# Attention and a mixture of experts on one core: some transposes of the probabilities moved from the DMA to TensorE

## The chip, the core and the metric

One core of a Trainium2 chip runs the whole program. The metric is the device time of one execution in microseconds, as the median of several runs. The engines that matter: TensorE (PE; its weight loads are listed as PEld), VectorE (DVE), ScalarE (ACT), GpSimd (POOL), and SyncE (SP), on whose queue all DMAs of the stage told of here are issued.

## The reference

```python
def _attn_ref(q, k, v, w1, b1, w2):          # B, H, S, D = 4, 8, 576, 64
    scores = scale * np.matmul(q, k.transpose(0, 1, 3, 2))
    ...                                      # a small network of the positions gives bias
    scores = scores + bias.transpose(2, 0, 1)[None, :, :, :]
    scores = scores - np.max(scores, axis=-1, keepdims=True)
    attn = np.exp(scores)
    attn = attn / (np.sum(attn, axis=-1, keepdims=True) + 1e-09)
    return np.matmul(attn, v).astype(np.float32)

def _moe_ref(x, w_gate, w1, w2):             # N, D, E, F = 2304, 512, 8, 1024
    logits = x @ w_gate
    logits = logits - logits.max()
    P = np.exp(logits)
    for _ in range(8):
        P /= P.sum(1, keepdims=True) + 1e-09
        P /= P.sum(0, keepdims=True) + 1e-09
        P *= N / E
    out = np.zeros((N, D), dtype=np.float32)
    for e in range(E):
        h = np.maximum(x @ w1[e], 0.0)
        ye = h @ w2[e]
        out += P[:, e:e + 1] * ye
```

## The kernel before, in words

The first part of the program computes the attention, the second the experts. The products run in pairs of f16 numbers (a high and a low half), so that the sums come out as in f32.

Attention goes by 16 **units**: one of the 4 batches with one of the 4 pairs of heads. The 576 query rows of a unit are five groups for each head: four tiles of 128 rows for each of the two heads, and one last tile that holds the 64 remaining rows of both. A unit is worked off in five **steps** (`unit_steps`): `gi` 0 and 1 are two pairs of tiles, once for each head `hh` (two tiles a step), and `gi` 2 is the last, fifth tile (one tile). The first four units do their steps of `gi` 0 first and then the rest; from the fifth unit on, a unit's five steps follow each other. There are 80 steps.

A step of two tiles does this. TensorE writes the scores of a tile into `s`, a PSUM tile of two buffers (`ps_s`). VectorE adds the bias and takes the maximum on the way to `sb` (tiles `br`, `bt` are the bias). ScalarE takes the exponential and its sum in place. `st_rcp` makes the reciprocal on VectorE. `st_hi` scales `sb` to f16 on ScalarE: the high half of `ah`. `st_lo` computes the low half on VectorE and issues the **DMA transpose** that turns `ah` (128 x 1152 for one tile, in blocks of 128 x 128: 9 blocks a tile) into `aT`. `ah` has 2 buffers, `aT` 3 for steps of two tiles, and 1 (`aT4`) for the fifth tile. Two steps after `st_lo` (`LAG`), `attend` multiplies `aT` with the values `vs` (or `xb`) into `pv`, from which ScalarE and VectorE make `xa`, `xb`, `xc`, the input of the experts.

Beside this run: loads of the next units' `nat` tiles, their cut into halves (`qk`, `vs`) and the transposes of `qk` on TensorE into `l` (`u_trans`, f16, identity `id16`), copied to `qkT`; and the first expert's matmuls, `l<-...,area`, which fill TensorE where it would wait.

What sets the order: every instruction of this part is recorded by `Engine` objects with a cost that the code estimates, and `Plan.emit` then writes them out by a list schedule over those costs: at each time the engine that is free first takes its ready work, in order of priority and then of the recording. `as_one` keeps a group together. Engines run their list in order. As every operation goes through one recording line, the profile shows L210 for all of them; tiles tell them apart. In the second part, a second plan does the same for the gate, the scaling of `P` and the experts.

Of the kernel before, what the change touches and what calls it, by code (L numbers as in the profile page):

```python
# [9 lines left out]
F16 = mybir.dt.float16  # L10
# [8 lines left out]
P = 128  # L19
B, H, S, D = 4, 8, 576, 64  # L20
NHP = H // 2
# [249 lines left out]
def attention_sinkhorn_moe(ctx, tc, q, k, v, w1, b1, w2, wg, m1, m2, xm, xm4, xf, sel, out):  # L271
# [11 lines left out]
    plan = Plan()  # L283
    vec, act, pool, pe, sync = (
        Engine(plan, e, n)
        for e, n in ((nc.vector, "dve"), (nc.scalar, "act"), (nc.gpsimd, "pool"), (nc.tensor, "pe"), (nc.sync, "dma"))
    )
# [15 lines left out]
    id16 = consts.tile([P, P], F16, name="id16")  # L303
# [109 lines left out]
    with ExitStack() as actx:  # L413
# [35 lines left out]
        def ps_s():  # L449
            return psA.tile([P, 1024], F32, name="ps_s", tag="s", bufs=2)  # L450
# [68 lines left out]
        for kind in range(1, 4):  # L519
            vec.scalar_tensor_tensor(  # L520
                out=wr,
# [8 lines left out]
            out=wa.rearrange("p g (j k) -> p (g j) k", j=4),  # L530
# [92 lines left out]
        def bias_step(between=()):  # L623
# [27 lines left out]
            out=w1r, in0=pw[:, H : H + 2], scalar1=s_wb[:, 0:1], scalar2=2.0**-11, op0=ALU.mult, op1=ALU.mult  # L651
# [5 lines left out]
            out=w2m,  # L657
# [22 lines left out]
        for i in range(2):  # L680
            r = slice(32 * i, 32 * i + 1)
# [113 lines left out]
        for n in range(8):  # L795
            for m in (2 * n, 2 * n + 1):
                nm, _, i = qk_order[m]
# [9 lines left out]
        with plan.urgent():  # L807
# [6 lines left out]
            out=c8, in0=u_qk[:, 0:1], scalar=0.125, in1=u_qk[:, 1:2], op0=ALU.mult, op1=ALU.mult  # L814
# [7 lines left out]
            out=g, in0=g0, scalar=s_qk[:, 0:1], in1=s_qk[:, 1:2], op0=ALU.mult, op1=ALU.mult  # L822
# [140 lines left out]
        def st_lo(s):  # L963
            n, ah = len(s["sb"]), s["ah"]
            s["aT"] = wrk.tile([P, 9 * n, P], F16, name="aT", tag="aT" if n == 2 else "aT4", bufs=3 if n == 2 else 1)
            for i, sb in enumerate(s["sb"]):
                vec.scalar_tensor_tensor(
                    out=ah[:, i, S:],
                    in0=sb,
                    scalar=s["st"][:, 3, i : i + 1],  # L970
                    in1=ah[:, i, 0:S],
                    op0=ALU.mult,
                    op1=ALU.subtract,
                )
            sync.dma_start_transpose(out=s["aT"], in_=ah.rearrange("p n s -> p (n s)"))

        def attend(u, gi, ss):

# [158 lines left out]
        for n in range(NS + LAG + 1):  # L1137
# [19 lines left out]
            if 0 < n <= NS:  # L1157
                s = steps[n - 1]
                st_hi(s)
                st_lo(s)  # L1160
                u, gi, hh = s["key"]
                groups.setdefault((u, gi), []).append(s)
                if gi == 2 or hh == 1:
                    due.append((n + LAG, u, gi, groups.pop((u, gi))))
# [21 lines left out]
        vec, act, pool, pe, sync = nc.vector, nc.scalar, nc.gpsimd, nc.tensor, nc.sync  # L1186
# [682 lines left out]
    for n, (e, b) in enumerate(seq):  # L1869
        r = visit[n]  # L1870
        i, at_end, leaves = (b, r % 2), n % 5 == 4, visit[n + 1 : n + 2] != [r]
# [96 lines left out]
```

## Time and profile before

| | us |
|---|---|
| median of 3 runs | 1784.25 |
| lowest, highest | 1779.7, 1787.0 |
| the profiled execution | 1784.56 |
| its span, first to last instruction | 1782.8 |

| engine | busy us | share of the span |
|---|---|---|
| PE | 1686.8 | 95% |
| DVE | 1447.8 | 81% |
| ACT | 1086.3 | 61% |
| POOL | 78.7 | 4% |

These shares are averages over two parts that have different limits. They are read by stage: the share of each engine and of the 16 DMA engines in stretches of the span, then the waits in the stretch in question, then the chain of work that ended last there. The attention part lasts until about 517 us, the experts take the rest.

### The profile page before, as it was taken

To read this page: it belongs to the slowest core of one execution; us is meant where nothing else is said; L and a number is where in the kernel's file an instruction comes from. 1 tells how busy PE (TensorE), PEld (TensorE's weight loads), DVE (VectorE), ACT (ScalarE), POOL (GpSimd) and SP (SyncE) were. 2 spreads that over 40 slices of the span, in tenths; PEclk is the share of its full clock that TensorE was granted. 3 is DMA by queue.
4 is the path that set the end of the run, shared out by engine and by line. 5 is a ranking of instruction groups with operands and counts; after the bars stand their busy time and mean duration, and the time that the engine had idled before them with its cause. 6 is when DMAs were issued, how large, how long until landed. Compare 5 with 4: busy or idle time off the path is not lost.

```text
span 1782.8 us, 40479 instructions
## 1 busy us (share of the span) xinstructions
PE 1686.8 (95%) x16640; PEld 1377.4 (77%) x16640; DVE 1447.8 (81%) x2627; ACT 1086.3 (61%) x1930; POOL 78.7 (4%) x90
## 2 busy tenths in 40 slices
PE   7887897898989999999999999999999999999998
PEld 4544564555666688888988898889888988898887
DVE  6898988898968898778887787878788878876666
ACT  7887888888856675545564555565555544453443
POOL 0120012122200000000000000000000000000000
PEclk9988799999999999999999999999999999999999
DMA  7769999999993164644473557445545653463321
GB/s 259 240 160 225 206 196 200 200 201 194 202 268 136 68 204 181 231 165 163 170 279 135 201 190 248 154 143 213 214 173 180 237 192 131 160 238 103 104 73 37
DMA packets 303358, 324.24 MB, mean 182 GB/s; under 512 B 191420, under 2 KB 231876, under 8 KB 298180
## 3 DMA queue, kind: packets, MB, share of 16 engines
q1 hardware_dynamic: 303172, 321.65, 60.0%
q8 instruction: 130, 2.13, 0.5%
q14 instruction: 56, 0.46, 0.1%
HBM read 189.86 MB, written 88.08 MB: 156 GB/s over the span
## 4 chain that ended last, share of the span: by engine, by line
PE 78%; DVE 8%; DMA 7%; ACT 3%; issue 2%; SPq 0%; DVEq 0%; ACTq 0%
PE bankA L1591 18%; PE bankA L1611 13%; PE bankE L1591 9%; PE bankE L1611 9%; PE bankB L1611 9%; PE l L210 6%; PE bankB L1591 4%; DMA aT<-ah 4%; PE s L210 4%; PE pv L210 3%; ACT area L210 2%; DVE ah L210 1%; DVE area L210 1%; DVE sb L210 1%; PE bankS L1427 1%
## 5 line engine op out<-in xcount | busy, mean ns | idle before, releaser
L1591 PEld LDWEIGHTS <-slot 128*128 128x128 f16 x5040 | 450.7, 98 | 48.3 <-issue 2.5
L1611 PEld LDWEIGHTS <-hA 128*128 128x128 f16 x2268 | 222.4, 98 | 27.1 <-issue 0.6
L210 PEld LDWEIGHTS <-area 128*128 128x128 f16 (+1 forms) x2477 | 155.2, 101 | 101.5 <-issue 33.2
L1591 PE MATMUL bankA<-xt,slot 128*128 128x256 f16 (+1 forms) x1680 | 186.1, 262 | 0.2 <-ACT u L1648 0.2
L1591 PE MATMUL bankE<-xt,slot 128*128 128x256 f16 (+1 forms) x1680 | 186.1, 262 | 0.0
L1636 ACT ACTIVATE hA<-c 128x512 f16<-128x512 f32 x189 | 118.0, 627 | 111.3 <-DVE c L1214 110.4
L1611 PEld LDWEIGHTS <-hS 128*128 128x128 f16 x1512 | 147.2, 98 | 22.2 <-ACT hS L1636 3.0
L1611 PEld LDWEIGHTS <-area 128*128 128x128 f16 x1512 | 148.0, 98 | 18.5 <-issue 1.4
L210 DVE SCALAR_TENSOR_TENSOR ah<-sb,st,ah 128x576 f16<-128x576 f32 x144 | 122.4, 876 | 24.1 <-ACT ah L210 23.9
L1214 DVE SCALAR_TENSOR_TENSOR hA<-c,hA 128x512 f16<-128x512 f32 x189 | 127.5, 685 | 12.3 <-ACT hA L1636 10.2
L1695 ACT COPY u<-bankA 128x512 f32<-128x512 f32 (+1 forms) x70 | 37.8, 540 | 157.6 <-PE bankA L1611 157.4
L210 ACT ACTIVATE ah<-sb,st 128x576 f16<-128x576 f32 x144 | 106.2, 770 | 37.6 <-DMA aT<-ah 33.5
L1648 ACT ACTIVATE u<-bankA 128x512 f32<-128x512 f32 x126 | 75.1, 596 | 67.6 <-PE bankA L1591 63.8
L210 ACT ACTIVATE sb<-sb,st 128x576 f32<-128x576 f32 x144 | 110.4, 769 | 7.4 <-DVE st L210 7.1
L210 PE MATMUL l<-area 128*128 128x512 f16 (+1 forms) x413 | 110.6, 385 | 3.5 <-ACT ys L210 0.4
L1214 DVE SCALAR_TENSOR_TENSOR acc<-c,fs,acc 128x256 f32<-128x256 f32 x252 | 110.6, 480 | 2.1 <-DMA out_dram<-acc 0.2
L210 PE MATMUL s<-qkT 128*128 128x512 f16 (+3 forms) x560 | 84.5, 302 | 23.0 <-DVE st L210 22.1
L1611 PE MATMUL bankA<-area,hS 128*128 128x256 f16 x756 | 88.6, 273 | 3.2 <-ACT hS L1636 2.5
L1611 PE MATMUL bankA<-area,hA 128*128 128x256 f16 x756 | 89.8, 276 | 0.0
L1611 PE MATMUL bankA<-area 128*128 128x256 f16 x756 | 88.2, 273 | 1.0 <-ACT u L1695 1.0
L1611 PE MATMUL bankE<-area,hS 128*128 128x256 f16 x756 | 88.5, 273 | 0.0
L1611 PE MATMUL bankB<-area,hA 128*128 128x256 f16 x756 | 88.2, 273 | 0.0
(239 smaller groups left out, 3155.6 us busy)
## 6 DMA issues: line engine op xcount, KB each, us to landing
sc_w<-stage SPq DMA_DIRECT2D x84, 512.0 KB
acc<-sc_y SPq DMA_DIRECT2D x102, 256.0 KB
area<-sc_w SPq DMA_DIRECT2D x48, 512.0 KB
sc_y<-acc SPq DMA_DIRECT2D x84, 256.0 KB
xt<-sc_t SPq DMA_DIRECT2D x18, 1024.0 KB
slot<-sc_w SPq DMA_DIRECT2D x36, 512.0 KB
bt<-sc_bias SPq DMA_DIRECT2D x26, 576.0 KB
raw<-in_moe_w_dram SPq DMA_DIRECT2D x28, 512.0 KB
```

Source lines behind the costliest of these rows:

```text
L210: self.plan.record(self.name, cost, lambda: fn(*args, **kw), ins, outs, move)
L1214: vec.scalar_tensor_tensor(out=o, in0=x, scalar=s, in1=y, op0=op0, op1=op1)
L1427: pe.matmul(r, id16 if sg > 0 else nid16, v[:, a, 2 * dq : 2 * dq + 2, tok * w : tok * w + w], start=(j == 0), stop=(j == len(seq_) - 1),)
L1591: pe.matmul(ps[:, jf * w : jf * w + w], t[:, a, c * 512 + f * P : c * 512 + f * P + P], x(xp, c), start=(first and jf == 0 and c == 0 and ...
L1611: pe.matmul(ps[:, j * 256 : j * 256 + 256], h[:, a, fc * w + j * P : fc * w + j * P + P], t[:, wp, fc * 256 : fc * 256 + 256], start=(firs ...
L1636: on_act(0.58, lambda: act.activation(h[:, 0, sl], x, AF.Relu if relu else AF.Copy), [r], wk)
L1648: on_act(0.55, lambda: act.activation(tmp[k], bank[b], f, scale=HS), [b], [k], 0)
L1695: on_act(0.27 * nt, lambda: act.copy(tmp[k][:, :n], bank[b][:, :n]), [b], [k], 0)
```

## The change

In `st_lo`, the DMA transpose stays only for some steps. For the fifth tile of every unit (`gi == 2`), and for the first four units' step with `(gi, hh) == (1, 1)`, whose two tiles are the last pair of the second head, each tile is transposed by nine matmuls with the identity into one buffer of `s` (taken as f16), and copied to `aT` by two instructions: ScalarE takes five blocks (640 columns), VectorE four (512 columns). That is 20 of the 80 steps and 24 tiles.

```diff
-            sync.dma_start_transpose(out=s["aT"], in_=ah.rearrange("p n s -> p (n s)"))
+            u, gi, hh = s["key"]
+            if not (gi == 2 or u < NHP and (gi, hh) == (1, 1)):
+                sync.dma_start_transpose(out=s["aT"], in_=ah.rearrange("p n s -> p (n s)"))
+                return
+            for i in range(n):
+                ps = ps_s().bitcast(F16)[:, : 9 * P].rearrange("p (r x) -> p r x", x=P)
+                with plan.as_one():
+                    for r in range(9):
+                        pe.transpose(ps[:, r], ah[:, i, r * P : (r + 1) * P], id16)
+                act.copy(s["aT"][:, 9 * i : 9 * i + 5], ps[:, :5])
+                vec.tensor_copy(s["aT"][:, 9 * i + 5 : 9 * i + 9], ps[:, 5:])
```

The plan orders everything behind the first such step anew. Three places show how. In the rows, the number behind a tile's name tells its buffer: `s_116` and `s_118` are the two of `s`.

TensorE, at the first unit's step `(1, 1)`, which is the first place where the orders part. Before, behind the last matmul of a `pv` group:

```order
L210 MATMUL pv_112<-aT_138,xb 64x256
L210 LDWEIGHTS qkT_129
L210 MATMUL s_116<-qkT_129 128x512
L210 LDWEIGHTS qkT_129
L210 MATMUL s_116<-qkT_129 128x64
```

Now, at the same place (nine transposes into each buffer, the repeats left out):

```order
L210 MATMUL pv_112<-aT_138,xb 64x256
L210 LDWEIGHTS ah_144
L210 MATMUL s_116<-id_68,ah_144 128x128
...
L210 LDWEIGHTS ah_144
L210 MATMUL s_118<-id_68,ah_144 128x128
...
L210 LDWEIGHTS qkT_129
L210 MATMUL s_116<-qkT_129 128x512
```

The scores that followed the `pv` group now stand behind 18 transposes, which use both buffers of `s` in turn.

VectorE at the same place, as a piece of the difference:

```order
 L210 ISA st_135 128x1
 L210 SCALAR_TENSOR_TENSOR xa<-pv_112,xa 128x256
+L210 COPY aT_124<-s_116 128x512
+L210 SCALAR_TENSOR_TENSOR area<-area,sms 128x1024
+L210 COPY aT_124<-s_118 128x512
 L210 ISA sb_141,st_139<-s_116,bt_123,sms 128x576
 L210 ISA st_139 128x1
 L210 ISA sb_133,st_139<-s_118,bt_123,sms 128x576
```

The two copies, with a cut of the first expert's weights between them, now stand ahead of the maxima (`ISA sb`) of the next scores, which use the same buffers.

SP, from the fourth unit's fifth tile through the fifth unit. Before:

```order
L210 DMA_TRANSPOSE aT_0_117<-ah_144 128x9x128
L210 DMA sc_y<-ys_108 128x512
L210 DMA bt_121<-sc_bias 128x1152
L210 DMA_TRANSPOSE aT_138<-ah_142 128x18x128
L210 DMA bt_123<-sc_bias 128x1152
L210 DMA_TRANSPOSE aT_122<-ah_144 128x18x128
L210 DMA sc_y<-ys_108 128x512
L210 DMA_TRANSPOSE aT_124<-ah_142 128x18x128
L210 DMA nat_119<-in_v_dram 64x2x64
L210 DMA nat_120<-in_q_dram 64x2x256 x2
L210 DMA_TRANSPOSE aT_138<-ah_144 128x18x128
```

Now:

```order
L210 DMA bt_121<-sc_bias 128x1152
L210 DMA_TRANSPOSE aT_122<-ah_144 128x18x128
L210 DMA bt_123<-sc_bias 128x1152
L210 DMA_TRANSPOSE aT_124<-ah_142 128x18x128
L210 DMA nat_119<-in_q_dram 64x2x256
L210 DMA_TRANSPOSE aT_138<-ah_144 128x18x128
L210 DMA sc_y<-ys_108 128x512
L210 DMA nat_119<-in_q_dram 64x2x256
L210 DMA nat_119<-in_q_dram 128x64
L210 DMA nat_120<-in_k_dram 128x576
L210 DMA_TRANSPOSE aT_122<-ah_142 128x18x128
```

The transposes of 9 blocks (`aT_0`) are gone from SP's list, the four of 18 blocks of the unit stay, and the loads between them have moved. From the gate matmuls at the end of the attention part on, the orders of all engines are the same.

## Rows read from the trace of the kernel before

**Rows 1.** The page's 40 slices of 44.6 us: busy tenths, DMA share in tenths.

```profile
PE   7887897898989999999999999999999999999998
...
DMA  7769999999993164644473557445545653463321
```

**Rows 2.** Stretches: length, PE, PEld, DVE, ACT, POOL busy (instructions), clock, DMA share, GB/s.

```profile
185.00:240.00 55.00, 47.83 (x459) 29.94 (x458) 51.43 (x108) 46.51 (x92) 7.08 (x7) 0.89 0.88 183
215.00:240.00 25.00, 24.40 (x259) 15.27 (x254) 22.62 (x49) 20.69 (x44) 5.44 (x4) 1.00 0.77 145
220.00:240.00 20.00, 19.40 (x194) 11.92 (x193) 19.23 (x39) 17.55 (x39) 5.44 (x4) 1.00 0.80 151
240.00:285.00 45.00, 42.44 (x412) 26.95 (x411) 38.84 (x89) 36.92 (x75) 9.22 (x11) 1.00 0.97 213
285.00:325.00 40.00, 28.07 (x277) 16.91 (x276) 34.60 (x80) 33.25 (x67) 7.34 (x9) 0.83 0.98 193
325.00:500.00 175.00, 161.69 (x1624) 104.62 (x1622) 156.09 (x348) 146.11 (x298) 35.63 (x35) 1.00 0.95 197
500.00:517.00 17.00, 15.64 (x178) 11.58 (x177) 6.14 (x9) 8.13 (x15) 0.00 (x0) 1.00 0.94 253
```

**Rows 3.** Waits, 240 to 500 us: engine, tile <- releaser: us in total, times, longest.

```profile
ACT ah L210 <- DMA aT<-ah: 21.1, 20, 2.2
DVE ah L210 <- ACT ah L210: 17.4, 17, 2.5
PE s L210 <- DVE st L210: 17.1, 22, 1.8
...
PE pv L210 <- DMA aT<-ah: 6.5, 7, 2.6
```

**Rows 4.** Chain that ended last, 185 to 517 us: by line, and one of its pieces (start, us).

```profile
by line: PE l L210 27.5%; DMA aT<-ah 23.1%; PE pv L210 13.9%; PE s L210 9.6%; DVE ah L210 6.0%; issue 4.8%; DVE sb L210 3.2%; ACT ah L210 2.3%; DVE area L210 2.1%; ACT sb L210 1.1%; DVE qk L210 0.9%; DVE st L210 0.8%; ACT area L210 0.8%; DV
...
268.65 5.04 DMA aT<-ah
```

**Rows 5.** Waits, 215 to 240 us, columns as in rows 3.

```profile
DVE ah L210 <- ACT ah L210: 0.9, 2, 0.8
...
ACT ah L210 <- DMA aT<-ah: 0.5, 1, 0.5
```

**Rows 6.** DMA transposes on SP's queue: all (ns), two small ones; 185-517 us traffic.

```profile
L210 SPq DMA_TRANSPOSE aT<-ah x80: 1253/3078/6224, 94.2 to 509.4; - x80
...
351.11 1.39 SPq L210 DMA_TRANSPOSE aT<-ah  x1
...
373.18 1.32 SPq L210 DMA_TRANSPOSE aT<-ah  x1
...
DMA packets 166760, 66.14 MB, mean 199 GB/s; under 512 B 155333, under 2 KB 160709, under 8 KB 166469
```

**Rows 7.** Prices: groups (count | busy us, mean ns | idle before), then TensorE in time.

```profile
L210 DVE TENSOR_TENSOR area<-l,area 128x512 f16<-128x512 f32 x26 | 17.7, 685 | 4.6 <-ACT area L210 4.6
L210 PE MATMUL l<-id,qk 128*128 128x128 f16 x216 | 18.1, 224 | 2.9 <-DVE area L210 1.8 <-ACT qkT L210 0.6 <-DVE qk L210 0.2
L210 ACT COPY qkT<-l 128x1024 f16<-128x1024 f16 x12 | 12.0, 1003 | 2.8 <-PE l L210 2.6 <-issue 0.2
L210 DVE COPY qkT<-l 128x1024 f16<-128x1024 f16 x12 | 8.2, 686 | 2.1 <-PE l L210 1.8
L210 ACT COPY qkT<-l 128x256 f16<-128x256 f16 x12 | 4.3, 358 | 0.9 <-PE l L210 0.9
...
263.18 0.61 PE L210 MATMUL l<-id,qk 128*128 128x128 f16 x8
263.63 1.04 PE L210 MATMUL l<-xa,area 128*128 128x256 f16 x8
...
302.29 0.99 PE L210 MATMUL l<-id,qk 128*128 128x128 f16 x8
303.12 1.11 PE L210 MATMUL s<-qkT 128*128 128x512 f16 x7
```

## The prediction

> **What bounds the kernel now.** I read the page's forty slices first, then a table of the run by stages, then the waits and the chain of the stage that the change touches. The run has two parts [rows 1]: attention until about 517 us, in which the DMA engines are almost always full, and the expert layers from there on, in which TensorE is full and the DMA half idle. The first transpose that the change moves stands behind the `pv` matmuls of about 182 to 185 us, and from the gate matmuls on (517 us) the instructions are the same in the same order, so all of the effect falls between 185 and 517 us. By stage [rows 2] the DMA share there is 0.88, then 0.97, 0.98 and 0.95, and no compute engine is far behind: over 185 to 500 us VectorE is busy for 51.43 + 38.84 + 34.60 + 156.09 = 281.0 of 315 us (89.2%), TensorE for 280.0 (88.9%), ScalarE for 262.8 (83.4%). Four resources within ten per cent of each other: a reader should see that taking load from the fullest one uncovers the next at once.
>
> Where the DMA holds the rest back is in the waits [rows 3]. `ah`, the f16 tile that is transposed, has two buffers; from 240 to 500 us ScalarE waits 20 times and 21.1 us for a transpose to release one, VectorE waits 17.4 us behind it for ScalarE's half of `ah`, and TensorE's `pv` waits 6.5 us for transposed tiles. The chain of 185 to 517 us agrees: 23.1% of it are transposes in flight, one of them 5.04 us [rows 4]. One stretch shows the stage without that pressure: 215 to 240 us, with the DMA at 0.77. There ScalarE waits 0.5 us for transposes, VectorE 0.9 us behind it [rows 5], and TensorE is busy for 24.40 of 25 us, VectorE for 22.62 [rows 2].
>
> **The change, part by part.**
>
> *Removed: 20 of 80 DMA transposes.* Sixteen have 9 blocks of 128 x 128, four have 18. On SP's queue the small ones take 1.39 and 1.32 us, and the middle of all 80 is 3.08 us, which is an 18-block one [rows 6]: 16 x 1.35 + 4 x 3.08 = 34 us. By bytes it is the same: 16 x 0.295 + 4 x 0.590 = 7.08 MB, at the 199 GB/s that the stage moves [rows 6], 35.6 us. The DMA's own work from 185 to 500 us, 0.88 x 55 + 0.97 x 45 + 0.98 x 40 + 0.95 x 175 = 297.5 us, falls to about 263, that is 0.85 of the stage as it forecasts below. So the DMA is no longer what paces it. The landing of a moved tile (about 5 us) is replaced by matmuls and copies worth 1 to 2 us, but nobody stood in line for most of these tiles, since `attend` comes two steps later.
>
> *Added on TensorE: 216 transposes in 24 groups of 9.* Eight such transposes of `qk` start at 263.18 and the next matmul starts at 263.63: 0.45 us for eight at full clock, so 0.51 us for nine, 24 x 0.51 = 12.2 us. At half clock eight take 0.83 us (302.29 to 303.12), which bounds the sum by 22.4 us [rows 7]. TensorE would then be busy for 292.2 us; in a stage of 309.5 us that is 94.4%, which it exceeds in the 215 to 240 us stretch. Its cover is thin, and it is the second thing to be late.
>
> TensorE's transposes bring in a rule of the Trainium skill that speaks against the change. The row first: eight took 0.45 us in this kernel, 56 ns apart [rows 7]. The page "TensorE: Matmul & The Clock Gate", section on PE-mode transpose, puts one 128 x 128 transpose in a kernel's context at about 275 ns, and says that such transposes don't hold up the engine's clock. By an estimate from that page the sum would be 216 x 275 ns = 59 us in place of 12.2.
>
> *Added on ScalarE: 24 copies of 640 columns out of PSUM.* The `qkT` copies of the same types take 1.003 us for 1024 columns and 0.358 us for 256 [rows 7]; on the line between them 640 columns take 0.68 us, 24 x 0.68 = 16.3 us. ScalarE has 21.1 us of waits for transposes to put it into; with all of it ScalarE stands at 279.1 us, 90% of the stage. I cost it at nothing beyond that, and at up to 0.68 us each where the `ah` waits don't go.
>
> *Added on VectorE: 24 copies of 512 columns.* Half of the 1024-column `qkT` copy (0.686 us) is 0.34, and I take 0.35: 8.4 us. The upper bound is the nearest row of the same width from PSUM, 0.685 us [rows 7]: 16.5 us. I take the lower since it is the same operation and type. It can't be below nothing, being new work. VectorE is the fullest compute engine, so this lies on the path.
>
> *Moved: buffers and queues.* The transposes are written into `s`, the two PSUM buffers that the scores use. The step's scores therefore stand behind a group of transposes in TensorE's order, and the buffer is free only when both copies are done. TensorE already waits 17.1 us in 22 waits for VectorE to free `s` from 240 to 500 us, 0.78 us each [rows 3]. On TensorE a group waits for VectorE's low half of `ah`, and behind it are queued the next scores and the expert matmuls `l`. On SP the loads that stood behind the removed transposes start earlier; they were not late, so I cost that at nothing (if the cover were gone, what waits is ScalarE's cut of `qk`). The tail, 500 to 517 us, is TensorE's `l` and `pv` [rows 2]; I leave it as it is.
>
> *The sum.* Once the DMA no longer paces the stage, VectorE does. Where it came nearest to that over a long stretch, 185 to 240 us, it was busy for 93.5% [rows 2]. With 281.0 + 8.4 = 289.4 us of work at 93.5% the 315 us become 309.5: 5.5 us less. With the dear copies it is 297.5 / 0.935 = 318.2, 3.2 us more. A second sum, from the waits, gives less: if VectorE's 17.4 us behind `ah` fall to the rate of 215 to 240 us (0.9 us in 25, so 9.4 in 260), it gains 8.0 and pays 8.4. The profiled execution took 1784.56 us, 1782.8 of it span, and stands 0.3 us from the median of 1784.25. Forecast: 1784.56 - 5.5 = 1779 us.
>
> **The rivals.** All bounds below are against 1784.25; 0.5%, or 8.9 us, is about what a measurement of this kernel can tell from no change.
>
> *The stage tightens more: faster.* With the DMA at 0.80, from 220 to 240 us, VectorE was busy for 19.23 of 20 us, 96.2% [rows 2]. If the whole stage ran so, 289.4 / 0.962 = 300.8 us, 14.2 less: 1770. For it: TensorE's clock was granted at 0.89 and 0.83 of full in two of the four stretches, the second one with 12 us of TensorE idle, and fewer stalls give some of that back. Against: TensorE would need 97%, and VectorE reaches that share in one short stretch only.
>
> *The `s` buffers take back more than the DMA gives: slower.* 24 groups claim one of two buffers that TensorE already waits for. If each costs a wait like the 22 seen, 0.78 us, that is 18.7 us, less the 5.5 gained: 13 more, 1798. It decides from (8.9 + 5.5) / 24 = 0.6 us a group. For it: behind each group stand scores on which VectorE's next maximum waits, and from 285 to 325 us, with no `l` to fill in, the cycle of scores and maxima is all there is. Against: where `l` matmuls stand next to a group, TensorE's lateness is covered. The same end follows if VectorE's idle share just stays as it is: 289.4 / 0.892 = 324.4, 9.4 more.
>
> *Each transpose is several times as dear: slower.* The 216 transposes of `qk` last 224 ns each from start to end [rows 7]. If the new ones don't overlap as those do, they cost 216 x 0.224 = 48.4 us; TensorE then needs 328.4 us, at the 97.6% of its best stretch 336.5, which is 21.5 more: 1806. The row of 0.45 us for eight speaks against it, and the clock was at full speed from 240 to 285 us with such transposes in it [rows 2, 7]. The rule of the page named above would end here too (by its figure, an estimate, at 339 / 0.976 = 347 us, some 1817); by that rule and its remark on the clock, the trace doesn't agree.
>
> That the change doesn't act isn't open: the order shows 60 DMA transposes in place of 80, and all 24 groups.
>
> **How the numbers follow.** The forecast (within 0.5%, 1775.4 to 1793.2) gets 0.48: both sums fall in it. Faster gets 0.35, for the best stretches are real. The buffers get 0.14, the dear transposes 0.03, together 0.17 for slower. The forecast's own range, between the two prices of VectorE's copy with a little for the clock, is 1774 to 1788. The range of 8 in 10 takes in most of the faster case (a few hundredths lie below 1765) and stops at 1794, short of the slower ones.
>
> **What would show it.** In the profile after: DMA share 0.80 to 0.88 from 240 to 490 us in place of 0.97; ScalarE's waits for `aT<-ah` down from 21.1 us to about 7; copies of `aT` at 0.68 and 0.35 us; groups of nine transposes at 0.5 us; the gate matmuls at 511 us in place of 517. The sum is wrong if VectorE's copies take 0.6 us, if its idle share stays at 11% with the DMA relieved (then something other than DMA paced it), or if TensorE's waits for `s` pass 30 us.

## The result, and the profile of the changed kernel

The changed kernel takes 1797.95 us (median of four runs, 1796.15 to 1801.12) against 1784.93 us: 1.0071 times as long, with an interval of 1.0046 to 1.0096. That is 13 us slower, and 4 us beyond 1794, the upper end of the range of 8 in 10. One of the four runs of d1_after_replan below took 2924.45 us at a mean granted clock of 0.556, where its others had 0.977; its figures leave that run out. The profiled execution took 1798.74 us, 1796.7 of it span, beside 1784.56 and 1782.8 before.

The stretches of the changed kernel, with the columns of [rows 2] (length, then busy time of PE, PEld, DVE, ACT and POOL, the clock, the DMA share, GB/s), show where it went:

```profile
185.00:240.00 55.00, 47.96 (x529) 32.48 (x527) 49.47 (x107) 48.37 (x90) 4.74 (x5) 0.98 0.51 130
240.00:285.00 45.00, 40.38 (x410) 26.67 (x406) 38.84 (x89) 39.61 (x80) 8.75 (x10) 0.94 0.81 184
285.00:325.00 40.00, 30.54 (x298) 18.26 (x297) 33.26 (x76) 31.07 (x63) 8.87 (x10) 0.86 0.80 161
325.00:500.00 175.00, 161.41 (x1620) 106.29 (x1620) 154.13 (x345) 146.71 (x296) 34.53 (x36) 0.97 0.86 182
...
531.00:1797.00 1266.00, 1247.79 (x11909) 1098.87 (x11907) 1006.66 (x1689) 673.48 (x1109) 0.00 (x0) 1.00 0.49 171
```

The DMA is relieved as forecast: 0.51, 0.81, 0.80 and 0.86 where [rows 2] have 0.88, 0.97, 0.98 and 0.95. The compute engines are hardly fuller for it. VectorE is busy for 275.7 of the 315 us from 185 to 500, where it was 281.0 [rows 2], although it has the new copies to do: it gets less of its old work done in the same time. TensorE has 280.3 us in place of 280.0, ScalarE 265.8 in place of 262.8, with most of its 16.4 us of new copies in that time. The granted clock, weighted by the length of the stretches, is 0.953 where it was 0.959, so the clock is hardly the difference. The stage simply ends later. The first gate matmul, which follows the attention part, starts here:

```profile
532.37 0.78 PE L1280 MATMUL bankS<-wgs,xa 128*128 128x8 f16 x25
```

Before, it started at 516.69 us. The 15.7 us between the two are all of the loss and somewhat more, since the profiled spans differ by 13.9; the expert part behind it takes 1264 to 1266 us in both.

The waits of the stage (engine, tile <- releaser: us in total, times, longest; changed kernel, 185 to 531 us) show in what form the time is lost:

```profile
PE s L210 <- DVE st L210: 17.9, 23, 2.4
ACT ah L210 <- DMA aT<-ah: 16.9, 18, 3.2
DVE ah L210 <- ACT ah L210: 15.8, 16, 3.6
DVE sb L210 <- PE s L210: 14.8, 18, 2.0
ACT aT L210 <- DVE aT L210: 10.8, 13, 1.8
ACT sb L210 <- DVE st L210: 6.6, 9, 1.9
```

Over the stage of the kernel before (185 to 517 us) the same view has:

```profile
ACT ah L210 <- DMA aT<-ah: 26.2, 24, 2.2
DVE ah L210 <- ACT ah L210: 23.9, 23, 2.5
...
PE s L210 <- DVE st L210: 21.7, 27, 2.1
```

ScalarE's waits for a transpose fell by 9.3 us and VectorE's behind it by 8.1, about as the second sum of the prediction had it. A new wait took their place: ScalarE's copy of a transposed tile stands 10.8 us behind VectorE's copy of the same tile. A piece of the timeline (start, us, engine, operation, idle before it) shows such a pair. In all 24 pairs of the trace the second copy starts when the first has ended, whichever engine comes first, so the 1.1 us of copying lie one behind the other:

```profile
363.47 0.42 DVE L210 COPY aT<-s 128x512 f16<-128x512 f16 x1 [1.04 <-PE s L210]
363.93 0.69 ACT L210 COPY aT<-s 128x640 f16<-128x640 f16 x1 [1.80 <-DVE aT L210]
```

The costs of the added groups (count | busy us, mean ns of one | idle before them):

```profile
L210 PE MATMUL s<-id,ah 128*128 128x128 f16 x216 | 18.4, 227 | 4.5 <-DVE ah L210 3.0 <-ACT ah L210 1.1 <-DVE st L210 0.4
L210 ACT COPY aT<-s 128x640 f16<-128x640 f16 x24 | 16.4, 689 | 13.2 <-DVE aT L210 10.8 <-PE s L210 2.3
L210 DVE COPY aT<-s 128x512 f16<-128x512 f16 x24 | 10.1, 422 | 6.8 <-PE s L210 5.2 <-ACT aT L210 1.5
```

### The profile page after: what moved, and what is told of

Read it like the earlier page. It is cut to its first block, busy times and chain, and to the rows that moved or that the text cites. A ratio compares the mean times of both kernels' runs of the same rounds, so it can differ in the third digit from the quotient of the medians.

```text
span 1796.7 us, 40856 instructions
## 1 busy us (share of the span) xinstructions
PE 1700.6 (95%) x16856; PEld 1390.0 (77%) x16856; DVE 1452.8 (81%) x2651; ACT 1101.7 (61%) x1954; POOL 77.5 (4%) x90
## 4 chain that ended last, share of the span: by engine, by line
PE 76%; DVE 10%; DMA 8%; ACT 3%; issue 2%; SPq 0%; DVEq 0%; ACTq 0%
PE bankA L1601 17%; PE bankA L1621 13%; PE bankB L1621 9%; PE bankE L1621 9%; PE bankE L1601 8%; PE l L210 6%; PE s L210 5%; PE bankB L1601 4%; DMA aT<-ah 4%; PE pv L210 3%; DVE ah L210 2%; DVE sb L210 1%; ACT area L210 1%; DVE area L210 1%; DMA xb<-in_moe_w_dram 1%
## 5 line engine op out<-in xcount | busy, mean ns | idle before, releaser
L1621 PE MATMUL bankE<-area,hA 128*128 128x256 f16 x756 | 88.6, 273 | 0.6 <-DVE hA L1224 0.6
L1621 PE MATMUL bankA<-area,hA 128*128 128x256 f16 x756 | 88.3, 273 | 0.0
```

What stands on the lines that cost most here:

```text
L1621: pe.matmul(ps[:, j * 256 : j * 256 + 256], h[:, a, fc * w + j * P : fc * w + j * P + P], t[:, wp, fc * 256 : fc * 256 + 256], start=(firs ...
```

## The experiments

Ratios are against the kernel before, on the same chip, with their interval.

### Parts of the change

**e1_fifth_only**, **e2_early_only**: only the 16 fifth tiles, or only the first four units' step (1, 1), go by TensorE.

```diff
-            if not (gi == 2 or u < NHP and (gi, hh) == (1, 1)):
+            if gi != 2:                                      # e1_fifth_only
+            if not (u < NHP and (gi, hh) == (1, 1)):         # e2_early_only
```

> Only the fifth tiles are transposed on TensorE (16 groups of nine), the first four units' pairs go back to the DMA. Theory A (each group costs, by holding a buffer of s and by two copies that run one behind the other): the loss goes by groups, 16/24 of 13 us = +9, about 1794 us. Theory B (the loss is of the new order as a whole, not of the groups): no such proportion; anything from 1780 to 1800. Theory C (the loss is made where the DMA had the most to give and the order changed most, in the first four units): near 1785.

> Only the first four units' steps (1, 1) are transposed on TensorE (8 groups of nine), all fifth tiles go by DMA. Theory A: 8/24 of 13 us = +4, about 1789 us. Theory B: no proportion. Theory C: near 1798, the whole loss.

Measured: 1799.29 us, 1.0081 [1.0054, 1.0107], and 1790.42 us, 1.0030 [1.0015, 1.0044]. Sixteen tiles lose as much as all 24, and the eight others alone lose 5 us. By the ratios the parts make 20 us where the whole has 13, which speaks against one price per tile, though only at the edge of what the intervals can tell. e2 alone lies where such a price (theory A) had it, e1 5 us above.

**e3_drop20**: the 20 transposes are left out and nothing is put in their place; the planner makes a new order.

```diff
-            for i in range(n):
-                ...
+            if (u, gi) == (0, 2):
+                pool.memset(s["aT"], 0.0)
```

> The 20 transposes are left out altogether: no DMA transpose, no matmuls, no copies (the fifth tiles then multiply zeros, the four pairs old values). It measures what taking them off the DMA is worth without paying for it. If the DMA paced the stage, as the prediction had it: 10 to 20 us faster than before, 1765 to 1775. If what held the stage was the latency of the transposes that stay (5 us each, with two buffers of ah), little comes: 1778 to 1785. Theory B allows even a slower one, since this order is new too.

Measured: 1788.17 us, 1.0017 [1.0002, 1.0031]. With a quarter of its transposes gone and nothing added, the kernel is not faster. That is above both ranges that were named for it; only the theory of the new order allowed it. The relief that the whole forecast hung on isn't there, at least not in this order.

**e4_l1_banks**: the blocks are transposed as five and four into the two buffers of `l`, so that each copying engine has a tile of its own and `s` is left alone.

```diff
-                ps = ps_s().bitcast(F16)[:, : 9 * P]...
+                for eng, lo, hi in ((act, 0, 5), (vec, 5, 9)):
+                    ps = psA.tile([P, 1024], F16, name="ps_t", tag="l1", bufs=2)...
```

> All 24 tiles on TensorE as in the change, but the nine blocks go as five and four into the two buffers of l, each copied by its own engine, so that s is left to the scores and the two copies no longer share a bank. Theory A: most of the loss goes, 1783 to 1789 us. If the work on VectorE and ScalarE itself is what costs, it stays at 1795 to 1800. Theory B: no bound.

Measured: 1810.34 us, 1.0142 [1.0119, 1.0166], slower still, and above every range named for it. (The transposes overwrite unfinished sums of the first expert, whose use of `l` goes by pairs of buffers; the work done is the same.) In its waits from 185 to 531 us, the copies no longer wait for each other, but for TensorE:

```profile
PE l L210 <- DVE area L210: 10.2, 5, 2.7
...
ACT aT L210 <- PE l L210: 6.2, 10, 1.2
...
DVE aT L210 <- PE l L210: 5.1, 7, 1.3
```

Where each has its own tile, they do run side by side:

```profile
238.10 0.69 ACT L210 COPY aT<-l 128x640 f16<-128x640 f16 x1 [0.59 <-PE l L210]
...
238.41 0.41 DVE L210 COPY aT<-l 128x512 f16<-128x512 f16 x1
```

That alone doesn't help: in place of `s`, the buffers of `l` are now held, and TensorE's `l` waits 10.2 us for one.

### The order held, and the order alone

**f1_held_drop19**: 19 of the 20 transposes are not issued, but the planner still counts them. Every other instruction therefore keeps its place in the order of the kernel before.

```diff
+            if not (gi == 2 or u < NHP and (gi, hh) == (1, 1)) or (u, gi) == (0, 2):
+                sync.dma_start_transpose(out=s["aT"], in_=src)
+                return
+            cost, *move = sync.transfer("dma_start_transpose", s["aT"], src)
+            plan.record("dma", cost, lambda: None, [src], [s["aT"]], move)
```

> The kernel before with its order held instruction by instruction, in which 19 of the 20 DMA transposes are simply not issued (all but the first unit's fifth tile; the tiles then hold old values) and nothing takes their place. It parts the relief of the DMA from the new order. If the DMA's load paces the stage (the prediction's step): 10 to 20 us faster than before, 1765 to 1775. If the pace is made elsewhere and the DMA is full only because it has that much to do: 1780 to 1786. The run that left the 20 out in a new order had 1788.

Measured: 1779.94 us, 0.9974 [0.9961, 0.9987], 5 us faster, at the faster edge of the range for a pace that is made elsewhere. Every engine's list in its trace is that of the kernel before, so this is the relief by itself, with nothing to pay. Two of its stretches, and its waits from 185 to 530 us:

```profile
185.00:240.00 55.00, 47.18 (x470) 29.65 (x466) 52.43 (x111) 48.57 (x94) 7.33 (x7) 0.93 0.56 138
240.00:500.00 260.00, 235.18 (x2354) 150.83 (x2354) 231.52 (x519) 218.61 (x444) 52.16 (x53) 0.98 0.90 189
```

```profile
PE s L210 <- DVE st L210: 21.3, 25, 2.1
DVE ah L210 <- ACT ah L210: 19.3, 19, 2.6
ACT ah L210 <- DMA aT<-ah: 16.5, 19, 2.3
```

VectorE is busy for 89.0% of the stretch; before, it was 88.3% (38.84 + 34.60 + 156.09 of 260 us [rows 2]). The DMA's share fell from 0.96 to 0.90 there, and from 0.88 to 0.56 from 185 to 240 us, where the four large transposes went; VectorE gained 1.0 us of the 55. ScalarE still waits 16.5 us (before 26.2) for transposes that remain. As 0.90 is still high, e3 and e3b, which add no work either, show the stage with more room, in new orders (240 to 500 us, e3 first):

```profile
240.00:500.00 260.00, 233.64 (x2290) 149.31 (x2289) 230.76 (x516) 217.32 (x443) 53.11 (x52) 0.95 0.85 183
```

```profile
240.00:500.00 260.00, 232.92 (x2262) 149.11 (x2261) 226.91 (x504) 213.45 (x435) 51.53 (x52) 0.95 0.86 183
```

With the DMA at 0.85 and 0.86, VectorE is busy for 88.8% and 87.3%. So a full DMA was not what kept VectorE from being busier, as far as runs in other orders can tell; the wait for a transpose that is still in flight stays.

**c1_replan**, **c2_replan**, **d1_after_replan**: no work is changed; one of the planner's cost numbers is, so that it writes another order. c1 and c2 are the kernel before, d1 the changed kernel with c1's number.

```diff
-            return (0.13 if ins and ins[0].space == PSUM else 0.16) + 0.03 * columns + n * 0.00097
+            return (0.13 if ins and ins[0].space == PSUM else 0.16) + 0.03 * columns + n * 0.00100
-            return 0.65, 0.165 * out.free_size() / P, 0.92          # c2_replan
+            return 0.65, 0.175 * out.free_size() / P, 0.92
```

> The kernel before with one number of the planner changed: its cost of ScalarE's work grows by 0.03 ns an element (0.00097 to 0.00100 us). No work is added or taken away, only the order is planned anew. Theory B (the loss is of the order): 1775 to 1800, away from 1785 by more than 4 us. Theory A (the loss is of the groups): within 4 us of 1785.

> The kernel before with another number of the planner changed: its cost of a block of a DMA transpose, 0.165 to 0.175 us. Again only the order is new. Theory B: away from 1785 by more than 4 us. Theory A: within 4 us of 1785.

> The changed kernel with the planner's number of c1 (0.00100). Theory A: slower than c1 by about the 13 us that the change costs, 1794 to 1800 if c1 is near 1785. Theory B: no such distance, it may lie on either side of c1 and of the 1798 of the change.

Measured: 1790.14 us, 1.0031 [1.0017, 1.0046]; 1794.08 us, 1.0047 [1.0030, 1.0064]; 1801.65 us, 1.0091 [1.0059, 1.0123]. A new order of the same work costs the kernel before 5 and 8 us. The two new orders tried are both slower than the one it has, and every change that lets the planner run again leaves that order. d1 lies 10.7 us above c1 by the ratios, beside the 12.7 of the change with the old number, so it comes near theory A's "about 13", which speaks against the new order as the whole loss.

One place shows a wait that an order brings. In the changed kernel TensorE waits here for VectorE's cut of a `qk`:

```profile
279.94 1.04 PE L210 MATMUL l<-id,qk 128*128 128x128 f16 x8 [4.01 <-DVE qk L210]
```

The kernel with nothing in place of the transposes (e3_drop20) has the same wait at the same place:

```profile
280.08 1.03 PE L210 MATMUL l<-id,qk 128*128 128x128 f16 x8 [3.12 <-DVE qk L210]
```

Between 255 and 305 us the kernel before has only one such wait, of 0.16 us. It comes with the new order and not with the added work.

### The copies

**h1_held_copies**: as f1, and at each of those places two copies of 512 columns on VectorE and one of 640 on ScalarE for each tile, from `ah` to `aT`, with no transposes on TensorE and no use of `s`. It is the copies' work alone, in the order held.

```diff
+            def copies():
+                for i in range(n):
+                    o = 1152 * i
+                    for _ in range(2):
+                        nc.vector.tensor_copy(aT[:, o : o + 512], src[:, o : o + 512])
+                    nc.scalar.copy(aT[:, o + 512 : o + 1152], src[:, o + 512 : o + 1152])
+            plan.record("dma", cost, copies, [src], [s["aT"]], move)
```

> The held order without the 19 DMA transposes, and in their place only the copies: for each of 23 tiles VectorE copies 512 columns of ah into aT twice (about 0.4 us in all) and ScalarE 640 columns once (about 0.7 us), from SBUF, without a transpose on TensorE and without touching s (the tiles then hold wrong values). Against the 1780 us of the run without them it prices the work of the copies alone. If the work is what the groups cost: 1787 to 1792. If it is the holding of s and the waits of one copy for the other: 1780 to 1784.

Measured: 1786.38 us, 1.0002 [0.9985, 1.0020]. That lies between the two ranges named for it. From 0.9974 to 1.0002 the copies' work took 5.0 us (1.1 to 8.9 by the two intervals), for this work:

```profile
L987 DVE COPY aT<-ah x46: 272/293/622, 188.1 to 510.2; 128x512 f16<-128x512 f16 x46
...
L988 ACT COPY aT<-ah x23: 703/719/740, 187.7 to 510.0; 128x640 f16<-128x640 f16 x23
```

That is 46 x 0.293 = 13.5 us on VectorE (3.4 more than the change has there) and 23 x 0.719 = 16.5 us on ScalarE (as many as the change). With the order held, relief and copying cancel. But these copies read SBUF, and they don't stand in line: 19 of ScalarE's 23 overlap one of VectorE's in time, though both read `ah` and write `aT`:

```profile
222.38 0.72 ACT L988 COPY aT<-ah 128x640 f16<-128x640 f16 x1
222.61 0.61 DVE L987 COPY aT<-ah 128x512 f16<-128x512 f16 x2
```

So it isn't the shared `aT` that puts the change's copies one behind the other.

**e5_act_copy**, **e6_dve_copy**: one engine copies all nine blocks.

```diff
-                act.copy(s["aT"][:, 9 * i : 9 * i + 5], ps[:, :5])
-                vec.tensor_copy(s["aT"][:, 9 * i + 5 : 9 * i + 9], ps[:, 5:])
+                act.copy(s["aT"][:, 9 * i : 9 * i + 9], ps)             # e5_act_copy
+                vec.tensor_copy(s["aT"][:, 9 * i : 9 * i + 9], ps)      # e6_dve_copy
```

> The change with ScalarE alone copying all nine blocks (1152 columns, by its two prices about 1.1 us): VectorE is spared its 24 copies, and no copy waits for the other. If VectorE's work and the wait of ScalarE behind it cost: 1790 to 1794. If ScalarE's time in line costs as much (its copy is 0.4 us longer, 10 us in all): 1797 to 1801. New order: +-5 on either.

> The change with VectorE alone copying all nine blocks (about 0.75 us). ScalarE is spared 16 us of copies and its 11 us of waits for VectorE's copy; VectorE has 8 us more. If VectorE is the bound: 1803 to 1808. If ScalarE's waits cost: 1790 to 1795. New order: +-5 on either.

Measured: 1810.90 us, 1.0130 [1.0102, 1.0158] with ScalarE; 1793.91 us, 1.0042 [1.0023, 1.0061] with VectorE. The copies of the two kernels (count: shortest/median/longest ns):

```profile
L210 ACT COPY aT<-s x24: 1096/1118/1125, 190.7 to 538.7; 128x1152 f16<-128x1152 f16 x24
```

```profile
L210 DVE COPY aT<-s x24: 750/757/764, 185.1 to 516.8; 128x1152 f16<-128x1152 f16 x24
```

ScalarE needs 24 x 0.361 = 8.7 us more for the same copies, and the kernel is 16 us (by the ratios) to 17 us (by the medians) slower, in one order each. e5 is 10 us above the dearer of its two ranges, e6 in the range for ScalarE's waits. The engine that the prediction took to be free is the worse place, and VectorE, the fullest compute engine, the better one.

**g1_plan_told**: the change, with the planner told that the copies come one behind the other (VectorE 0.42 us, then ScalarE 0.69).

```diff
+                for eng, op, lo, hi in ((vec, "tensor_copy", 5, 9), (act, "copy", 0, 5)):
+                    ...
+                    plan.node(eng.name, 0.42 if eng is vec else 0.69, fn, [region(x)], [region(o), region(x)])
```

> The change with the planner told what the trace shows: VectorE's copy first at 0.42 us, ScalarE's behind it at 0.69 us, since two copies of one bank of s never ran side by side. The work is the same. If a wrong plan of these copies is what costs: 1788 to 1793. If the order is a matter of luck: 1790 to 1805, like the change and its other order (1798, 1802).

Measured: 1805.72 us, 1.0095 [1.0058, 1.0132], in single runs from 1796 to 1808, just above both ranges named for it. A planner that knows of the wait found no better order here.

### Two orders of each kernel

As one order says little, five kernels were compared in two orders each, the second with the planner's ScalarE number at 0.00100. (The same number doesn't make the same order in two kernels.) **i1_no_copies** and **i2_no_copies_replan** keep TensorE's 24 groups in `s`, but VectorE copies a single column of each; **e3b_drop20_replan** and **e6b_dve_replan** are e3 and e6 in the second order.

```diff
-                act.copy(s["aT"][:, 9 * i : 9 * i + 5], ps[:, :5])
-                vec.tensor_copy(s["aT"][:, 9 * i + 5 : 9 * i + 9], ps[:, 5:])
+                vec.tensor_copy(s["aT"][:, 9 * i, :1], ps[:, 0, :1])    # i1, i2
```

> The change with its 24 groups of transposes into s, but only one column of each copied, by VectorE (the fifth tiles then multiply zeros, the pairs old values). If TensorE's transposes and the holding of s cost by themselves: 1793 to 1798, near the change, and 5 to 10 above the run that leaves the transposes out (1788). If it is the copies' work and waits, on top of a new order: 1786 to 1790.

> The same with the planner's number of c1 and d1 (0.00100): a second order. If s costs: 5 to 10 above e3b. If not: within 4 of e3b.

> The 20 transposes left out, with the planner's number of c1 (0.00100). If a new order costs 5 to 8 us whatever it is, and the relief is worth 5: 1785 to 1789. If orders are luck: anything from 1775 to 1795.

> VectorE alone copies all nine blocks, with the planner's number of c1. If sparing ScalarE is what made 1794 out of 1798: 4 to 8 below d1 (1802), 1794 to 1798. If 1794 was the order: 1799 to 1806.

| | first order | second order | mean | us over the first row |
|---|---|---|---|---|
| before | 1 | 1.0031 (c1) | 1.0016 | 0 |
| 20 transposes left out | 1.0017 (e3) | 1.0001 (e3b) | 1.0009 | -1 |
| TensorE's transposes, one column copied | 0.9982 (i1) | 1.0035 (i2) | 1.0009 | -1 |
| copied by VectorE alone | 1.0042 (e6) | 1.0051 (e6b) | 1.0047 | 6 |
| the change | 1.0071 | 1.0091 (d1) | 1.0081 | 12 |

(The last column is the difference of the means times 1785 us.) One kernel's two orders lie up to 9 us apart (i1, i2: 1782.56 and 1793.36 us, by their ratios 9.5). A single step of 6 us between two rows is therefore weak, and the first row owes its 0 to the one order that was there: with c2 as a third order its mean is 1.0026, and the change stands 10 us above it. The 13 us between the third row and the last are stronger: they are 16 us in the first order and 10 in the second. TensorE's transposes by themselves cost nothing that can be told from the orders' spread: i1 is 6 us faster than e3, and i2 is 6 us slower than e3b, which is where its expectation had put a cost of `s`. What the last row adds to the third is the copies at full width, the waits of one for the other, and the 1.1 us for which both keep a buffer of `s`, where i1 and i2 free it after one column. These three weren't parted by a run. The trace of the change gives a small figure for the last: from 185 to 531 us TensorE waits 2.1 us for a copy to free `s`.

```profile
PE s L210 <- ACT aT L210: 1.5, 2, 0.8
...
PE s L210 <- DVE aT L210: 0.6, 2, 0.4
```

The other side of `s` is VectorE, which waits for scores that stand behind the transposes: 7.3 us from 185 to 517 us in the kernel before, 14.8 in the changed one. The same wait in i1, then in i2 (185 to 530 us):

```profile
DVE sb L210 <- PE s L210: 15.0, 21, 1.7
```

```profile
DVE sb L210 <- PE s L210: 21.0, 25, 3.2
```

i1 has as long a wait as the changed kernel and is no slower than the kernel before, so the wait alone doesn't make the loss. i2 has a longer one and is 6 us slower, so a part of it is not excluded.

## Why the prediction was wrong

*What held.* The DMA's shares (0.80 to 0.88 forecast, 0.80 to 0.86 measured from 240 to 500 us). TensorE's 216 transposes: a group of nine starts at 236.03 us in the changed kernel and the next matmul at 236.54, 0.51 us, as worked out:

```profile
236.03 0.67 PE L210 MATMUL s<-id,ah 128*128 128x128 f16 x9
...
236.54 1.46 PE L210 MATMUL l<-area 128*128 128x512 f16 x6
```

The rival with dear transposes falls. i1 and i2 with all 216 are no slower on the mean than e3 and e3b without them. The Trainium skill (page "TensorE: Matmul & The Clock Gate", section on PE-mode transpose) gives about 275 ns for one transpose in a kernel's context. As the length of one that is near the 227 ns here; as a price for each, which the prediction's estimate took it for, it doesn't agree with the trace, since nine overlapped and took 0.51 us. ScalarE's copy was sized right (0.689 us, 0.68 forecast). The second sum, from the waits, came out at nothing, and with the order held so did the runs: relief gives 5 us (it said 8.0) and the copies' work takes 5.0 (it said 8.4 for VectorE's). That is partly luck, as each term measured about 60% of its forecast and h1's copies are not the change's. From 240 to 500 us ScalarE's waits for transposes fell to 12.0 us, not to 7.

*First failed step: "so the DMA is no longer what paces it", and VectorE then at 93.5%.* The DMA's full share was taken for the limit of the stage, and the stretch from 215 to 240 us for a picture of the stage without it. Without the copies the same sum gives 281.0 / 0.935 = 300.5 us, a relief of 14.5; f1 had 5. There VectorE's share from 240 to 500 us goes from 88.3% to 89.0%, not to 93.5%, and e3 and e3b have no more with the DMA at 0.85. What ScalarE waits for is one transpose in flight with `ah` in two buffers, and that still takes about 3 us (2.98 us, the median in f1). That this latency sets the pace is argued from the waits: no run gave `ah` a third buffer. The prediction had named an idle share that stays as a rival's end ("if VectorE's idle share just stays as it is", 9.4 us more, which is 1794) and as a sign that something other than the DMA paced the stage, and gave it too little.

*Second failed step: ScalarE's 16.3 us of copies "at nothing".* Waits are not a place to put work, unless the work is ready when the wait is. The copies come where TensorE's groups end, and ScalarE's ends up behind VectorE's (10.8 us, a wait that the prediction didn't have at all), while the scores' exponentials and the halves of `ah` stand behind it in ScalarE's order. Leaving ScalarE out (e6, e6b) saves about 6 us on the mean of two orders, a weak step by itself, although VectorE then has 18.2 us of copies in place of 10.1; giving it all (e5, one order) costs 15 more than that. In h1, where the copies run side by side, 13.5 us on VectorE and 16.5 on ScalarE cost 5.0 together, so the copying time alone doesn't make them dear. What does in the change, their place in the order, their wait or their reading PSUM, no run parts.

*Third failed step: the new order at nothing.* The prediction priced the loads on SP that moved, and not that everything behind 185 us is planned anew. c1 and c2 price that at 5 and 8 us for the same work. Between f1 and the two orders of the kernel without the 20 (which also leave out one transpose more) lie 7.7 us (e3) and 4.8 (e3b). It is a spread and no fixed price: i1 has a new order too and is 1.4 us above f1.

*A mis-sized term.* VectorE's copy took 0.422 us instead of 0.35, 10.1 us instead of 8.4. That is 1.7 us and explains little.

*The slower rival had the time and not the reason.* It gave 1798 through TensorE's waits for `s`. Those behind VectorE's `st` fell slightly (21.7 to 17.9 us over the stage), those behind the copies are 2.1 us, and i1 and i2 show no cost of the groups in `s` on the mean, with 6 us to either side.

*The sum as it stands now:* relief -5 and the copies' work +5 with the order held (f1, h1); the other 12 to 13 us lie between h1 and the change. c1, c2 and the steps from f1 to e3 and e3b make 5 to 8 us for a new order likely, and the step from e6 to the change about 6 for ScalarE's copy behind VectorE's. These two are not measured apart in one order, so how the 12 us divide between them stays open. Also open is why two copies of one tile of `s` run one behind the other: the trace shows that one releases the other, e4 that copies from two tiles of PSUM can overlap, and h1 that a shared `aT` doesn't prevent it; copies from two banks of one tile weren't tried. None of the kernels that do the whole work beats the kernel before.

## What to carry to other kernels

A resource that is 95% full isn't thereby the bound: take its load away with the order of everything else held, and see what that gives, before you pay another engine to relieve it. A wait in another engine's list is a price for what ends it, not free room; what counts is whether the new work is ready then and what is queued behind it. Where a planner writes the order, a change of the work also redraws the order, so compare in several orders, and hold the order where an edit allows it.

## What the runs showed of the hardware

Copying out of PSUM in f16 cost ScalarE 1.118 us for 1152 columns and VectorE 0.757; for VectorE the same 512 columns took 0.422 us from PSUM and 0.293 from SBUF, while ScalarE's 640 took 0.689 and 0.719.

A transpose of 18 blocks got little quicker with less beside it. Of those behind 180 us the median is 3.16 us before (57 of them) and 2.95 in f1 (53), where 19 of 80 are gone; in the changed kernel it is 3.30 (52), though the DMA share there is 0.84 from 240 to 500 us. The rows of all transposes of f1 and of the changed kernel (shortest/median/longest ns):

```profile
L210 SPq DMA_TRANSPOSE aT<-ah x61: 2429/2980/6410, 93.6 to 499.7; - x61
```

```profile
L210 SPq DMA_TRANSPOSE aT<-ah x60: 2491/3313/5502, 95.3 to 520.6; - x60
```
